# Two more tiles turned on VectorE in the first half of layer 0

## The chip, the cores and the metric

The kernel runs on one core of one Trainium2 chip. The metric is the device time of one execution in microseconds (us); lower is better. Times of the kernel before are the median of three runs.

## What is computed

Two layers, each a linear-attention block and an MLP with residuals, on 2048 tokens of width 448 in float32 (16 heads of 28, hidden width 1792):

```python
x = x + A(layernorm(x), wqkv, wo)      # A: phi(t) = where(t > 0, t + 1, exp(t)) + 1e-6
x = x + B(layernorm(x), w1, b1, w2, b2)  #   kv = phi(k)^T v, z = sum phi(k)
x = x + A(layernorm(x), wqkv, wo)      #   o = (phi(q) kv) / (phi(q) z + 1e-6), then @ wo
x = x + B(layernorm(x), w1, b1, w2, b2)  # B: gelu(x @ w1 + b1) @ w2 + b2
```

## The kernel before

The 2048 tokens are 16 tiles of 128. Products keep float32's accuracy by splitting each operand into a high and a low part ("hi" and "lo", XH and XL for the normalised input) and adding three products. A layer has a first half (a pass over the 16 tiles that makes the keys, the queries and the sum G), a transition, and a second half (queries and MLP in blocks of four tiles). The change touches the first half of layer 0 only.

Instructions are issued in an order written out by hand: for each tile t, `STEPS` gives a string of tokens, or else `STEP`, and `phase1` issues what each token names, on whichever engines it needs. Every engine works off its own queue in that order. The tokens:

- `qp`: phi of the queries made a step earlier (ScalarE relu and exp into eq, VectorE adds, L372; then a store to memory by SP). `K`, `Q`: the products for keys and queries of tile t, 11 matmuls each on TensorE (L353). `Q` is issued in the first half for tiles up to 8.
- `a`, `n`: layer norm of a later tile: statistics (VectorE L209, L221, L214, then GpSimd's power brs, L215) and normalisation (VectorE L442).
- `T`: where a tile's transposition is on TensorE, the four transposes of tile t+1 into PSUM (L264). For these tiles `stage_n` also copies the tail of the row (ScalarE, L446).
- `v` with a number, or `tu`: where it is on VectorE, `turn` transposes the tile in 32x32 squares (L303, L304) into a buffer that holds two tiles. After the odd one, SP stores the pair to memory (`store_sq`, L310). `sp`: SP spreads each stored pair back into SBUF by four DMAs (L318), so that the squares come to lie where a full transpose would have put them.
- `X`: split of tile t+1 into XH (ScalarE) and XL (VectorE): from PSUM `split_x` (L276, L277), from the spread squares `split_t` (L335, L336).
- `s`: split of the normalised tile itself, the stationary side of G (ScalarE xnh L477, GpSimd xnl L478 and a short L479).
- `kp`, `kh`, `kl`: phi of the keys (ScalarE ek L369, L370, VectorE L372), its high part (ScalarE L517), its low part and the running sum za (VectorE L526, L533).
- `G`: the 11 matmuls of tile t-1 into G (L622). `bg`: casts of MLP weights that were loaded a step earlier (ScalarE w1h, w1x; GpSimd w1l), then loads of the next pieces by SP. `ld`: the load of a later x tile by SP.

`TURNED[l]` is the first tile of layer l that VectorE turns; tiles below it use TensorE's transposes. It is 8 in layer 0 and 0 in layer 1. `k_at`, `q_at` and `g_at` say at which of the 11 places the matmuls with the low part stand, so that they come when that part is there; `merge` puts the list together. The psk and tp/psq banks come in pairs ("m" and "h", two buffers each), used in turn; the buffers for stored and spread squares and some weight pieces are five of one kind ("S").

Of the kernel before, what the change touches and what calls it, by code (L numbers as in the profile page):

```python
# [22 lines left out]
def linear_attn_mlp_kernel(  # L23
# [12 lines left out]
    pe, act, dve, pool, sp = nc.tensor, nc.scalar, nc.vector, nc.gpsimd, nc.sync  # L36
# [8 lines left out]
    G = 112  # L45
# [37 lines left out]
    def load_x(l, t):  # L83
        xt[l, t] = t448("H", 8, f"x{l}_{t}")
        sp.dma_start(xt[l, t], x_d[l][t * 128:(t + 1) * 128, :])
# [166 lines left out]
    def block(key):  # L252
        if key not in blocks:
            blocks[key] = Block(APART if key[0] == "a" else 0)
        return blocks[key]
# [3 lines left out]
    def transpose_x(xn, tail, key, j, tag="m"):  # L259

        block(key)
        tp = tps[key, j] = bank(tag, 4 if tag == "acc" else 2, "tp")
        for c in range(4):
            pe.transpose(tp[:, c * 128:(c + 1) * 128], xn[:, c * 128:(c + 1) * 128] if c < 3 else tail, ident)  # L264
# [8 lines left out]
    def split_x(key, j):  # L273
        tp = tps.pop((key, j))
        hi, lo = blocks[key].pieces(j)
        act.copy(hi, tp)  # L276
        dve.tensor_sub(lo, tp, f(hi))  # L277
# [20 lines left out]
    def turn(x, key, t):  # L298
        x = x[:, :D]
        if (key, t // 2) not in squares:  # L300
            squares[key, t // 2] = half("sq")
        sq = squares[key, t // 2].rearrange("p (m c u n) -> p c m u n", m=4, c=4, n=32)[:, :, :, t % 2]
        dve.transpose(sq[:, :3], x[:, :TL].rearrange("p (c m n) -> p c m n", c=3, n=32))  # L303
        dve.transpose(sq[:, 3].rearrange("p (u m) n -> p u m n", u=2),  # L304
                      x[:, TL:].rearrange("p (m n) -> p m n", n=32)[:, None].to_broadcast([128, 2, 2, 32]))
# [70 lines left out]
    def bg_pieces():  # L376
        n = 0
        both = []

        def stage():  # L380
            nonlocal n
            n += 1
            if n <= LATE:
                k = (n - 1) // 2
                if k % 2 == 0 or k > 5:
                    return t512("xn", 2, "stg")[:, :D]

                if n % 2:
                    both.append(half("stg"))
                return both[-1][:, n % 2 * 512:][:, :D]  # L390
            return t448(f"W{5 + n % 2}", 1, "stg")

        for fc in range(4):
            sl = slice(fc * D, (fc + 1) * D)
            for c in range(4):
                s = stage_piece(w1[:, sl], c, sp, stage())

                def go(c=c, s=s, sl=sl):
                    if c < 3:
                        act.copy(w1h[:, c, sl], s)  # L400
                        pool.tensor_tensor(w1l[:, c, sl], s, f(w1h[:, c, sl]), op=OP.subtract)
                    else:
                        act.copy(w1x[:, sl], s)
                        pool.tensor_tensor(w1x[64:128, sl], s[64:128], f(w1x[64:128, sl]), op=OP.subtract)
                yield go
        for i in range(NF):
            s = stage()
            sp.dma_start(s, w2[i * 128:(i + 1) * 128, :])

            def go(i=i, s=s):  # L410
                act.copy(w2h[:, i], s)
                pool.tensor_tensor(w2l[:, i], s, f(w2h[:, i]), op=OP.subtract)
            yield go

    bg = bg_pieces()
# [14 lines left out]
    sts = {}  # L430


    TURNED = (8, 0)
    tails = {}

    def stage_a(l, t):
# [2 lines left out]
    def stage_n(l, t):  # L439
# [3 lines left out]
        xns[l, t] = xs  # L443
        if t < TURNED[l]:
            d = tails[l, t] = b2b[:, t % 2 * 128:][:, :128]
            act.copy(d.rearrange("p (u n) -> p u n", u=2), xs[:, None, TL:].to_broadcast([128, 2, 64]))  # L446

    def stage_t(l, t):
        if t >= TURNED[l]:
            turn(xns[l, t], ("a", l, t // 4), t % 4)  # L450
            if t % 2:
                store_sq(("a", l, t // 4), t % 4 // 2)

    def stage_sp(l, t):
        if t >= TURNED[l]:
            block(("a", l, t // 4))
            spread(("a", l, t // 4), t % 4 // 2)

    def stage_b(l, t, tag="h"):
        if t < TURNED[l]:  # L460
            transpose_x(xns[l, t], tails.pop((l, t)), ("a", l, t // 4), t % 4, tag)
# [4 lines left out]
    def stage_x(l, t):  # L466
        key = ("a", l, t // 4)
        if t < TURNED[l]:
            split_x(key, t % 4)
# [13 lines left out]

    def k_at(l, t):
        if t < 9:
            return (3, 6, 9, 11) if t == 0 or l == 0 and 2 < t < 8 else (2, 5, 8, 11)
        return (2, 5, 8, 11) if t == 9 else (1, 4, 7, 10)

    def q_at(l, t):
        if t < 9:  # L490
            return (2, 5, 8, 11) if l == 0 and t < 7 else (2, 4, 7, 10) if t == 0 else (1, 4, 7, 10)
        return {11: (4, 7, 10, 11), 12: (5, 7, 9, 11),
                13: (5, 8, 10, 11), 15: (1, 5, 8, 11)}.get(t, (1, 4, 7, 10))

    def g_at(l, t):
        if t < 9:
            return (4, 7, 10) if l == 0 and 0 < t < 6 else (3, 6, 9)
        return (2, 5, 8) if t < NT - 1 else (2, 6, 9)

    def stage_k(l, t, cs=range(4)):  # L500
        ko[l, t] = proj("k", ("a", l, t // 4), t % 4, ko.get((l, t)), cs, k_at(l, t))
# [47 lines left out]
    def stage_q(l, t, cs=range(4), tag=None):  # L549
        if tag:  # L550
            qs_[l, t] = bank(tag, 4, "psq")[:, :D]
        qs_[l, t] = proj("q", ("a", l, t // 4), t % 4, qs_.get((l, t)), cs, q_at(l, t))
        if 3 in cs:
            qo.append((l, t, qs_.pop((l, t))))
# [33 lines left out]
    def stage_qphi(n=9):  # L588
        for _ in qo[:n]:
            l, t, o = qo.pop(0)  # L590
            if (l, t) == (0, 0):
                by_rs(o)

            e = phi(o, "eq", tag="e" if t < NT - 2 else "E")
            sp.dma_start(pq_d[l][t * 128:(t + 1) * 128, :], e)

    def fill_qphi():

        l, t, o = qo.pop(0)
        e = t512("e", 3, "eq")[:, :D]  # L600
        p = t512("E", 2, "ep")[:, :D]
        act.activation(e, o, AF.Relu, scale=-1.0)
        act.activation(p, o, AF.Relu)
        act.activation(e, e, AF.Exp, scale=-1.0)
        pool.tensor_tensor(e, p, e, op=OP.add)
        sp.dma_start(pq_d[l][t * 128:(t + 1) * 128, :], e)

    def stage_g(l, t, acc, mid=lambda: None):
        h, lo = split.pop((l, t))
        kh, kl = ks.pop((l, t))  # L610
        first, last = t == 0, t == NT - 1
        x = [h[:, c * 128:(c + 1) * 128] for c in range(3)] + [h[:, TL:]]
        his = [(c, x[c], k) for c in range(4) for k in (kh, kl)]
        if t == NT - 3:
            his = his[::2] + his[1::2]
        los = [(c, lo[:, c * 128:(c + 1) * 128], kh) for c in range(3)]
        made = merge(his, los, g_at(l, t))
        for i, (c, w, k) in enumerate(made):
            if i == 3:
                mid()  # L620
            others = [m[0] for m in made[:i]], [m[0] for m in made[i + 1:]]
            pe.matmul(acc[c], w, k, start=first and c not in others[0], stop=last and c not in others[1])  # L622
# [17 lines left out]
    STEPS = {  # L640
# [9 lines left out]
    }  # L650
    NORM = (
# [122 lines left out]
    def trans_gt(tr, acc):  # L774
        tr.gt = []
        for c in range(4):
            s = t512("A" if c < 2 else "B", 2, "gt")[:, :D]
            act.copy(s, acc[c])
            tr.gt.append(s)
# [52 lines left out]
    def load_pq(l, b, j):  # L832
        t = b * 4 + j
        pqt[l, t] = t448(f"W{j}", 1, f"pq{l}_{t}")
        sp.dma_start(pqt[l, t], pq_d[l][t * 128:(t + 1) * 128, :])
# [280 lines left out]
    for l in range(LAYERS):  # L1116
# [11 lines left out]
        def pre(j):  # L1128
# [6 lines left out]
            Q=lambda j: stage_q(l, fill.pop(0)), Qp=lambda j: fill_qphi(), Qv=lambda j: stage_qphi(j or 9),  # L1135
# [3 lines left out]
            ld=lambda j: (load_pq(l, 0, j), load_x(l, j)), gt=lambda j: trans_gt(tr, acc),  # L1139
# [14 lines left out]
        for b in range(NB):  # L1154
# [6 lines left out]
            for i in range(NF):  # L1161
# [12 lines left out]
                elif l + 1 < LAYERS:  # L1174
# [4 lines left out]
                    if i in (3, 4, 6, 7, 8):  # L1179
                        t = (3, 4, 6, 7, 8).index(i)  # L1180
# [36 lines left out]
```

## Time and profile before

| | us |
|---|---|
| median of 3 runs (866.61 to 866.7) | 866.67 |
| the profiled execution | 866.77 |
| span of its trace | 865.0 |
| TensorE busy | 859.5 (99%) |
| VectorE busy | 489.9 (57%) |
| ScalarE busy | 354.0 (41%) |
| GpSimd busy | 209.1 (24%) |

The page names TensorE PE (its weight loads PEld), VectorE DVE, ScalarE ACT, GpSimd POOL and the DMA queue of SyncE SPq. Times in a timeline are from the start of the span. The granted TensorE clock was at full speed in all slices. The first half of layer 0 lies at about 7 to 105 us.

### The profile page before, as it was taken

Reading aid. Unit: us, or ns where it says so; the run is one execution under the profiler, and the core shown is the slowest. Engines: PE = TensorE matmul, PEld = TensorE weight load, DVE = VectorE, ACT = ScalarE, POOL = GpSimd, SP = SyncE. Lnnn points to the kernel's source line nnn. Section 1 sums busy time; section 2 is a strip of 40 time slices with the busy share of each in tenths; the row PEclk is TensorE's granted clock in tenths of the full one; section 3 lists DMA queues with packets and bytes.
Section 4 is the critical chain, followed back from the end, with each engine's and each line's share of the span. In section 5 each row is a group of like instructions: output and inputs, shape, how many; then the busy total and the mean of one; then the engine's idle time right before and its main releaser. Section 6 shows DMA issues by size and latency. Waiting matters only on the chain.

```text
span 865.0 us, 11671 instructions
## 1 busy us (share of the span) xinstructions
PE 859.5 (99%) x4173; PEld 769.9 (89%) x4173; DVE 489.9 (57%) x956; ACT 354.0 (41%) x634; POOL 209.1 (24%) x242
## 2 busy tenths in 40 slices
PE   9999999999999999999999999999999999999998
PEld 8999988888888888888899998988888888888887
DVE  7888676559455443236477877664674383533112
ACT  6776656333323322333356565632232233223231
POOL 3565612235013012012222343120220140140000
PEclk9999999999999999999999999999999999999999
DMA  5475546633313502051145543362332423111001
GB/s 168 131 241 178 187 112 206 194 112 109 135 60 114 150 0 98 1 182 49 49 149 187 164 129 97 108 217 81 116 107 91 135 74 114 50 49 42 1 1 43
DMA packets 65082, 95.81 MB, mean 111 GB/s; under 512 B 9088, under 2 KB 59904, under 8 KB 65024
## 3 DMA queue, kind: packets, MB, share of 16 engines
q1 hardware_dynamic: 63696, 94.13, 33.8%
q10 hardware_dynamic: 1328, 0.93, 0.4%
q8 instruction: 33, 0.54, 0.3%
q14 instruction: 25, 0.20, 0.1%
HBM read 56.70 MB, written 35.13 MB: 106 GB/s over the span
## 4 chain that ended last, share of the span: by engine, by line
PE 95%; ACT 2%; DMA 1%; DVE 1%; issue 0%; POOL 0%; ACTq 0%; SPq 0%; DVEq 0%
PE hp L972 31%; PE y L1002 10%; PE y L1001 10%; PE y L1003 10%; PE G L622 8%; PE psk L353 8%; PE psq L353 5%; PE op L891 2%; PE op L890 2%; PE op L892 2%; DMA sp<-sq_m 1%; PE op L880 1%; PE op L879 1%; PE op L881 1%; PE kvp L786 1%; PE mp L796 1%
## 5 line engine op out<-in xcount | busy, mean ns | idle before, releaser
L978 DVE TENSOR_TENSOR gl<-g,gh 128x512 fp32r<-128x512 f32 x112 | 83.2, 743 | 293.2 <-ACT gh L977 293.2
L974 ACT ACTIVATE g<-hp,b1s 128x512 f32<-128x512 f32 x112 | 77.1, 688 | 400.1 <-PE hp L972 400.1
L1002 PE MATMUL y<-w2l,gh 128*128 128x448 f32 x447 | 163.6, 366 | 0.0
L1001 PE MATMUL y<-w2h,gh 128*128 128x448 f32 x447 | 162.2, 363 | 0.0
L1003 PE MATMUL y<-w2h,gl 128*128 128x448 f32 x447 | 160.3, 359 | 0.1
L972 PE MATMUL hp<-XH,w1h 128*128 128x512 f32 x336 | 130.7, 389 | 0.0
L972 PE MATMUL hp<-XH,w1l 128*128 128x512 f32 x336 | 130.7, 389 | 0.0
L972 PE MATMUL hp<-XL,w1h 128*128 128x512 f32 x336 | 130.1, 389 | 0.0
L215 POOL TENSOR_TENSOR brs<-bve,mhalf 128x1 f32<-128x1 f32 x55 | 34.8, 632 | 258.4 <-DVE bve L214 257.9
L1001 PEld LDWEIGHTS y<-w2h,gh 128*128 128x128 f32 x447 | 83.7, 187 | 9.8 <-ACT gh L977 0.5
L1002 PEld LDWEIGHTS y<-w2l,gh 128*128 128x128 f32 x447 | 83.9, 188 | 6.9
L1003 PEld LDWEIGHTS y<-w2h,gl 128*128 128x128 f32 x447 | 84.0, 188 | 5.8 <-DVE gl L978 0.9
L972 PEld LDWEIGHTS hp<-XL,w1h 128*128 128x128 f32 x336 | 63.1, 188 | 13.1
L972 PEld LDWEIGHTS hp<-XH,w1h 128*128 128x128 f32 x336 | 63.0, 187 | 10.7
L972 PEld LDWEIGHTS hp<-XH,w1l 128*128 128x128 f32 x336 | 63.1, 188 | 9.9
L977 ACT CAST gh<-g 128x512 fp32r<-128x512 f32 x112 | 69.6, 622 | 3.6
L840 POOL TENSOR_TENSOR pz<-pq,zb 128x448 f32<-128x448 f32 x32 | 37.0, 1162 | 103.3 <-DVE dn L846 67.1
L353 PE MATMUL psk<-wk,XH 128*128 128x448 f32 x210 | 61.8, 364 | 0.0
L353 PE MATMUL psq<-wq,XH 128*128 128x448 f32 x196 | 57.5, 366 | 0.0
L478 POOL TENSOR_TENSOR xnl<-x,xnh 128x384 fp32r<-128x384 f32 x32 | 35.0, 1092 | 69.3 <-ACT xnh L477 56.0
L622 PE MATMUL G<-kh,xnh 128*128 128x448 f32 x128 | 46.8, 368 | 0.0
L336 DVE TENSOR_TENSOR XL<-sp,XH 128x512 fp32r<-128x512 f32 x54 | 45.3, 851 | 2.1 <-ACT XH L335 2.1
(185 smaller groups left out, 1491.1 us busy)
## 6 DMA issues: line engine op xcount, KB each, us to landing
x<-in_A_x_dram SPq DMA_DIRECT2D x32, 224.0 KB, 3.7
pq_d<-eq SPq DMA_DIRECT2D x32, 224.0 KB, 2.7
pq<-pq_d SPq DMA_DIRECT2D x32, 224.0 KB, 3.1
sq_m<-sq SPq DMA_DIRECT2D x14, 512.0 KB, 2.6
x<-x_d SPq DMA_DIRECT2D x32, 224.0 KB, 3.7
sp<-sq_m SPq DMA_DIRECT2D x52, 128.0 KB, 2.8
sq_a<-sq SPq DMA_DIRECT2D x12, 512.0 KB, 2.9
sp<-sq_a SPq DMA_DIRECT2D x48, 128.0 KB, 2.7
```

Of the source, the lines that this page charges most:

```text
L336: eng.tensor_tensor(lo.rearrange("p (c i n) -> p c i n", c=4, n=32), x, f(h), op=OP.subtract)
L353: pe.matmul(o, x, p, start=(i == 0), stop=(i == 10))
L478: pool.tensor_tensor(lo[:, :TL], xn[:, :TL], f(h[:, :TL]), op=OP.subtract)
L622: pe.matmul(acc[c], w, k, start=first and c not in others[0], stop=last and c not in others[1])
L840: pool.tensor_tensor(pz, pqt[l, b * 4 + j], tr.zb, op=OP.mult)
L972: pe.matmul(o, w, r, start=(k == 0), stop=(k == len(made) - 1))
L974: act.activation(g, hp, AF.Gelu_apprx_tanh, bias=b1s[:, i:i + 1])
L977: act.copy(gh, g)
L978: dve.tensor_sub(gl, g, f(gh))
L1001: pe.matmul(acc[j], gh[:, s], w2h[:, i], start=first, stop=False)
L1002: pe.matmul(acc[j], gh[:, s], w2l[:, i], start=False, stop=False)
L1003: pe.matmul(acc[j], gl[:, s], w2h[:, i], start=False, stop=stop)
```

## The change

`TURNED` of layer 0 goes from 8 to 6, so tiles 6 and 7 are turned by VectorE, stored and spread, and TensorE's four transposes for each of them and the two tail copies go. The bounds in `k_at`, `q_at` and `g_at` move with it: tiles 6 and 7 in K, 5 and 6 in Q, and 4 and 5 in G take the positions that the later tiles have. The steps of tiles 3 to 11 are written anew. Normalisation of tiles 6 and 7 and statistics of tile 8 change places within steps 3 and 4, so that 6 and 7 can be turned at the end of step 3. The turns of tiles 9 to 15 each come a step later, and the spreads move with the stores. In steps 5 to 8 `X`, the split of the next tile, stands behind `s`, and in all of steps 5 to 11 ahead of `kp`. In steps 6, 9, 10 and 11 a turn stands directly ahead of `kp`, in steps 7 and 8 directly behind it.

```diff
-    TURNED = (8, 0)
+    TURNED = (6, 0)
...
     def k_at(l, t):
         if t < 9:
-            return (3, 6, 9, 11) if t == 0 or l == 0 and 2 < t < 8 else (2, 5, 8, 11)
+            return (3, 6, 9, 11) if t == 0 or l == 0 and 2 < t < 6 else (2, 5, 8, 11)
...
     def q_at(l, t):
         if t < 9:
-            return (2, 5, 8, 11) if l == 0 and t < 7 else (2, 4, 7, 10) if t == 0 else (1, 4, 7, 10)
+            return (2, 5, 8, 11) if l == 0 and t < 5 else (2, 4, 7, 10) if t == 0 else (1, 4, 7, 10)
...
     def g_at(l, t):
         if t < 9:
-            return (4, 7, 10) if l == 0 and 0 < t < 6 else (3, 6, 9)
+            return (4, 7, 10) if l == 0 and 0 < t < 4 else (3, 6, 9)
...
     STEP = "qp K T X s a kp n kh kl tu G bg Q ld sp"
     STEPS = {
         (0, 1): "T X a3 q1 s kh n3 kl q1 G bg ld",
         (0, 2): "K T X s a4 kp n4 a5 kh kl n5 a6 G bg Q ld",
-        (0, 3): "qp K T X s a7 kp kh n6 kl a8 G bg Q ld",
-        (0, 4): "qp K T X s a9 kp kh n7 n8 kl n9 v8 v9 G bg Q ld sp",
-        (0, 8): "qp K T X s a kp n kh kl tu a14 G bg Q ld sp",
-        (0, 9): "qp K T X s kp n14 kh kl v14 G bg",
-        (0, 10): "K T X s a15 kp n15 kh kl v15 G bg sp",
-        (0, 11): "K T X kp s kh kl G bg",
+        (0, 3): "qp K T X n6 s a7 kp kh n7 kl v6 v7 G bg Q ld sp",
+        (0, 4): "qp K T X s a8 kp kh n8 a9 kl v8 n9 G bg Q ld",
+        (0, 5): "qp K s X kp kh v9 a10 kl n10 G bg Q ld sp",
+        (0, 6): "qp K s X v10 kp kh a11 kl n11 G bg Q ld",
+        (0, 7): "qp K s X kp v11 kh a12 kl n12 G bg Q ld sp",
+        (0, 8): "qp K s X kp v12 kh a13 kl n13 a14 G bg Q ld",
+        (0, 9): "qp K X s v13 kp n14 kh kl G sp bg",
+        (0, 10): "K X s v14 kp a15 kh kl n15 G bg",
+        (0, 11): "K X v15 kp s kh kl G sp bg",
         (1, 0): "K T X s kp kh kl a n tu Q ld sp",
     }
```

## The prediction

> **What bounds the kernel now.** I read the page first, then TensorE's waits over the whole run, then the chain that ended last through layer 0's first half, then the timelines of the engines and queues around tiles 3 to 14.
>
> ```profile
> PE 859.5 (99%) x4173; PEld 769.9 (89%) x4173; DVE 489.9 (57%) x956; ACT 354.0 (41%) x634; POOL 209.1 (24%) x242
> PE warm L170 <- DVE one L164: 1.1, 1, 1.1
> PE psk L567 <- ACT wk L137: 0.8, 1, 0.8
> ```
>
> The first line is the page's busy time; the other two are all of TensorE's waits. TensorE bounds the kernel. Its only waits, 1.1 and 0.8 us, lie in the launch, ahead of everything that the diff touches. So there is no idle time for the change to remove: it can only take TensorE work away, or bring a wait in.
>
> ```profile
> 42.98 0.44 PE tp L264 x4
> 43.41 2.21 PE G L622 x11
> 45.62 2.20 PE psq L353 x11
> 50.03 0.44 PE tp L264 x4
> 50.47 2.21 PE G L622 x11
> ```
>
> These are pieces of the chain (start, us, what). Between K, G and Q pieces of 2.2 us stand the four transposes of tile 6 (42.98, in step 5) and of tile 7 (50.03, in step 6), 0.44 us each, with nothing idle around them.
>
> **What is removed.** Both pieces go: 2 x 0.44 = 0.88 us of TensorE, all on the path. That is the whole possible gain, and 0.10% of the run. Differences within 0.2% (1.7 us) count as no change here, about what a measurement of this kernel can tell. The matmuls' changed order inside K, Q and G keeps their number and shapes, so it costs nothing by itself. ScalarE also loses the two copies of the tails (about 0.2 us of queue each).
>
> **What is added.** Each tile is now turned in squares on VectorE, stored, spread back by four DMAs, and split from SBUF instead of PSUM.
>
> ```profile
> 42.48 0.57 DVE L303 STREAM_TRANSPOSE sq<-x 128x384 f32<-128x384 f32 x1
> 43.82 0.58 DVE L372 SCALAR_TENSOR_TENSOR eq<-psq,eq 128x448 f32<-128x448 f32 x1
> L336 DVE TENSOR_TENSOR XL<-sp,XH 128x512 fp32r<-128x512 f32 x8 | 8.2, 1027 | 0.8 <-ACT XH L335 0.8
> L277 DVE TENSOR_TENSOR XL<-tp,XH 128x512 fp32r<-128x512 f32 x5 | 3.4, 683 | 0.8 <-ACT XH L276 0.8
> 74.47 1.02 POOL L478 TENSOR_TENSOR xnl<-x,xnh 128x384 fp32r<-128x384 f32 x1
> 74.60 1.43 DVE L336 TENSOR_TENSOR XL<-sp,XH 128x512 fp32r<-128x512 f32 x1
> ```
>
> Two tiles were turned from 42.48 to 43.82, 0.67 us each, so VectorE gains 1.34 us. The groups between 20 and 105 us show an XL from SBUF at 1027 ns on average against 683 from PSUM. The last two lines say why: XL of tile 11 began just after GpSimd's xnl and ended 0.54 us after it (76.03 against 75.49). I take "held until GpSimd is done" as a hazard of up to 1.43 - 0.65 = 0.8 us for each such operation. In steps 5 to 8 xnh now stands ahead of the next tile's XH, so xnl starts some 0.6 us before XL, and a hold becomes the rule.
>
> The TensorE work is gone for certain; the cost is whether operands still arrive in time. I follow the new queue order through three places.
>
> **Place 1: step 3, the bank for Q of tile 4.**
>
> ```profile
> 31.10 0.68 DVE L277 TENSOR_TENSOR XL<-tp,XH 128x512 fp32r<-128x512 f32 x1
> 31.54 1.02 POOL L478 TENSOR_TENSOR xnl<-x,xnh 128x384 fp32r<-128x384 f32 x1
> 31.70 0.62 DVE L209 BATCH_NORM_STATS2 bst<-x 128x6 f32<-128x448 f32 x1
> 32.64 0.62 DVE L372 SCALAR_TENSOR_TENSOR psk<-psk,ek 128x448 f32<-128x448 f32 x1
> 33.17 0.50 DVE L442 TENSOR_SCALAR x<-x,bmv,brs 128x448 f32<-128x448 f32 x1
> 33.29 0.64 ACT L517 ACTIVATE kh<-psk,tiny 128x448 fp32r<-128x448 f32 x1 [0.77 <-DVE psk L372]
> 33.96 0.62 DVE L526 SCALAR_TENSOR_TENSOR kl<-psk,kh 128x448 fp32r<-128x448 f32 x1 [0.29 <-ACT kh L517]
> 35.03 0.62 DVE L209 BATCH_NORM_STATS2 bst<-x 128x6 f32<-128x448 f32 x1
> 35.53 0.58 ACT L370 ACTIVATE eq<-eq 128x448 f32<-128x448 f32 x1
> 36.14 0.62 DVE L372 SCALAR_TENSOR_TENSOR eq<-psq,eq 128x448 f32<-128x448 f32 x1
> 38.40 0.37 PE L353 MATMUL psq<-wq,XH 128*128 128x448 f32 x1
> ```
>
> The order was XL4, statistics of 7, phi of 3, n6, kl3, za, statistics of 8, eq; it becomes XL4, n6, statistics of 7, phi of 3, n7, kl3, za, turns of 6 and 7, eq. n6 would start at 31.70, where xnl runs until 32.56; held, it ends at about 33.0. The statistics take 32.64 - 31.70 = 0.94, so phi starts at 33.94, 1.3 us late (0.45 if n6 isn't held). kh and all of ScalarE behind it shift by that, less the tail copy: the exp that ended at 36.11 ends at about 37.2. n7 fits into the wait for kh. kl starts at 35.27, kl and za take 35.03 - 33.96 = 1.07, two turns 1.34: eq starts at 37.68 and ends at 38.30, where it ended at 36.76. Q of tile 4 reuses, by the two-bank rotation, the bank that this eq reads, and starts at 38.40. So 1.64 us of cover become 0.1: cost 0, up to 0.3 if something slips. Statistics of 8 move from step 3's end into step 4 and change VectorE's total by nothing.
>
> **Place 2: tile 6 by way of memory, and G of tile 5.**
>
> ```profile
> 79.78 0.27 DVE L304 STREAM_TRANSPOSE sq<-x 128x128 f32<-128x128 f32 x1
> 80.08 0.32 SPq L310 DMA_DIRECT2D sq_a<-sq  x1
> 83.03 1.76 SPq L318 DMA_DIRECT2D sp<-sq_a  x4
> 87.37 0.62 ACT L335 CAST XH<-sp 128x512 fp32r<-128x512 f32 x1 [0.88 <-DMA sp<-sq_a]
> 88.02 0.69 DVE L336 TENSOR_TENSOR XL<-sp,XH 128x512 fp32r<-128x512 f32 x1 [0.79 <-ACT XH L335]
> 47.66 0.56 PE L353 MATMUL psk<-wk,XH 128*128 128x448 f32 x2
> 50.51 0.36 PE L622 MATMUL G<-kl,xnh 128*128 128x448 f32 x1
> DMA to landing us min/median/max: 2.5/2.9/3.8
> 31.58 0.47 SPq L103 DMA_DIRECT2D stg<-in_B_w_dram  x1
> 40.46 0.56 ACT L403 CAST w1x<-stg 128x448 fp32r<-128x448 f32 x1
> 44.34 1.15 SPq L101 DMA_DIRECT2D stg<-in_B_w_dram  x2
> 47.54 0.57 ACT L400 CAST w1h<-stg 128x448 fp32r<-128x448 f32 x1 [0.39 <-DMA stg<-in_B_w_dram]
> ```
>
> Tiles 14 and 15 price the detour: store issued at 80.08, four spreads at 83.03, XH of tile 14 released at 87.37: 7.29 us. The new store goes out at 37.7, so XH of tile 6 can start at 45.0 and XL ends at 46.3, or 47.1 if held. K of tile 6 moves from 47.66 to 47.22 and fits. Behind that XH stands ek of tile 5 (0.5 for XH, 1.15 for relu and exp): phi of 5 at 46.65, then on VectorE phi 0.53, turn of 9 0.67, statistics of 10 0.94, kl 0.62: ends at 49.4. G of tile 5 wants kl at 50.51 - 0.88 = 49.63. Cost 0 to 0.25 (with XL held).
>
> On SP the store stands ahead of the loads that went out from 31.58, so these now leave after 38.0; such a load took 47.54 - 44.34 = 3.2 us, and ScalarE's w1x cast slides from 40.46 to about 41.9, the w1h cast behind it to 42.6, and eq of tile 4 behind both is ready at 44.2 (0.47 for the cast, 1.15 for relu and exp). VectorE comes to that eq at 44.0: 37.68, then eq 0.6, XL 0.65, statistics of 8 0.94, phi 0.53, n8 0.45, statistics of 9 0.94, kl and za 1.07, turn 8 0.67, n9 0.45. So it costs 0.2 of VectorE's time and nothing on TensorE; were VectorE on time as before, it would be more. By the same sum kl of 4 ends at 42.4, ahead of its G, which moves from 43.41 to 42.97. The x loads behind are used a step or more later.
>
> **Place 3: steps 9 to 13, XL of tile 14.**
>
> ```profile
> 76.73:81.15 4.42, 4.42 (x24) 4.13 (x23) 4.20 (x10) 3.17 (x6) 2.03 (x3) 1.00 0.07 27
> 89.97 0.37 PE L353 MATMUL psk<-wk,XL 128*128 128x448 f32 x1
> ```
>
> Without Q a step is 4.42 us, and VectorE (third busy time of the windows' line) fills 4.20 of it. Here turns 13, 14 and 15 come a step later, and turn 15 now stands behind XL of tile 12 instead of ahead of it. Turn 15 ended at 80.05; XL of 14 ended at 88.71, 8.66 later, and K of 14, which starts with XL, came at 89.97: cover 1.26. Now TensorE comes at 89.09. Following the order with 0.65 for an XL, 0.67 a turn, 0.94 statistics and the ScalarE waits as before, turn 15 ends at 80.1; with one hold of 0.8, at 81.0. XL of 14 then ends at 88.75 to 89.65: TensorE waits 0 to 0.55.
>
> **The sum.** Waits do not add: one at an early place moves the later needs back. So -0.88 and 0 to 0.55; I take 0.1, near the lower end, because the larger one needs a hold just there. The profiled execution took 866.77 (span 865.0 and 1.77 around it), 0.10 above the median 866.67. 866.77 - 0.88 + 0.1 = 866.0 there, 865.9 as median.
>
> **Rivals.** (A) The detour is slower than tiles 14 and 15 show. Landings went from 2.5 to 3.8 around a median of 2.9, so store and spread could come up to 1.8 later together; with 1.5, phi of 5 starts at 48.15, kl ends at 50.9, and G of 5 waits 1.27: 866.67 - 0.88 + 1.27 = 867.1. For it: ScalarE's queue holds ek of 5 behind XH of 6. Against: no transposed tile's data was late but the last pair's, by 0.88 of ScalarE's time.
>
> (B) VectorE becomes the bound in steps 9 to 11, and the run is slower. Place: XL of 10, 11, 12 and n14, n15, held by GpSimd, 0.8 each: 4.0 us, turn 15 at 84.1. K of 14 then waits 84.1 + 8.66 - 89.09 = 3.67: 869.5. It starts to cost when turn 15 ends after 80.43, and makes the run slower by over 0.2% when it ends after 83.04. For it: 4.20 of 4.42 us busy, and 1.34 us more work upstream with 0.88 us less time. Against: the 4.20 hold such delays already (XL of 11 alone 0.8), and before step 9 VectorE still has gaps. The Trainium skill speaks for (B)'s side: VectorE: DVE Perf Modes, sections "The three transpose paths" and "Rules for kernel authors", has VectorE turn only 32x32 blocks and sends a full 128x128 transpose to TensorE. By that rule 0.44 us of TensorE are the cheaper way and the result is a loss such as (B)'s, not a gain of 0.88; the rows agree about the detour's 7.29 us, not yet that it ends up on the path.
>
> (C) Faster by over 0.2%: needs 0.85 us beyond the removed pieces, and no wait of TensorE is there to remove.
>
> That the change does not remove the transposes is excluded: in the built kernel's order tiles 6 and 7 have none.
>
> **Chances and range.** Forecast 0.56 (865.8 to 866.4), (A) 0.18, (B) 0.24, (C) 0.02. The forecast and (A) lie within 0.2%: 0.74; slower 0.24; faster 0.02. (B) is given more than the replay alone bears, since the cover is at 0.1 to 0.5 us in four places and I follow queues by hand. The range goes from 865.6 (all 0.88, and the 0.1 by which runs differ on both sides) into (B), to 868.6.
>
> **What would show it.** Right: the chain has no tp pieces at 43 and 50, K of tile 12 starts 0.6 to 0.9 earlier, TensorE's list has at most 0.6 us of new waits, on XL of 14, on kl of 5 or on eq ahead of Q of 4. Store of 6 and 7 near 37.7, XH of 6 near 45.0, turn 15 ending by 81. Wrong: a wait of over 1 us on XL or kl between 38 and 95, turn 15 after 83, or a wait at a place not named.

## The result and the profile after

| | before | after |
|---|---|---|
| median of nine runs (us) | 866.70 (866.44 to 867.34) | 869.41 (867.09 to 870.59) |
| the profiled execution (us) | 866.77 | 870.35 |
| its span (us) | 865.0 | 868.5 |

The ratio after to before is 1.0025, 95% interval 1.0013 to 1.0036: slower, by 2.7 us in the medians. A later set of eleven runs (a2, below) gave 867.94 against 867.03, ratio 1.0013 [1.0004, 1.0023]. The runs of the changed kernel spread over more than 3 us, those of the kernel before over 0.9 us.

The page's busy times of after, and then all of TensorE's waits (what waited, for what; us in total, times, longest):

```profile
PE 860.4 (99%) x4165; PEld 769.2 (89%) x4165; DVE 492.4 (57%) x960; ACT 353.0 (41%) x632; POOL 210.4 (24%) x242
```

```profile
PE psk L353 <- DVE XL L336: 2.0, 2, 1.6
PE warm L170 <- DVE one L164: 1.1, 1, 1.1
PE psk L567 <- ACT wk L137: 0.7, 1, 0.7
PE G L622 <- DVE kl L526: 0.5, 1, 0.5
```

The eight transposes are gone (4165 matmuls for 4173). In their place stand three waits that before did not have: on the keys' low part of tile 5 and twice on XL, 2.5 us together. The timeline of after shows these places and what stands behind them on ScalarE and VectorE (start, us, engine, line; in brackets the idle time before it and who ended it; the first three lines are TensorE's):

```profile
50.83 0.47 PE L622 MATMUL G<-kl,xnh 128*128 128x448 f32 x1 [0.45 <-DVE kl L526]
73.31 0.47 PE L353 MATMUL psk<-wk,XL 128*128 128x448 f32 x1 [0.40 <-DVE XL L336]
93.10 0.47 PE L353 MATMUL psk<-wk,XL 128*128 128x448 f32 x1 [1.63 <-DVE XL L336]
46.30 0.62 ACT L335 CAST XH<-sp 128x512 fp32r<-128x512 f32 x1 [1.13 <-DMA sp<-sq_a]
71.80 0.62 ACT L335 CAST XH<-sp 128x512 fp32r<-128x512 f32 x1 [2.11 <-DMA sp<-sq_a]
80.94 0.62 ACT L335 CAST XH<-sp 128x512 fp32r<-128x512 f32 x1 [1.09 <-DMA sp<-sq_a]
91.70 0.62 ACT L335 CAST XH<-sp 128x512 fp32r<-128x512 f32 x1 [3.26 <-DMA sp<-sq_a]
92.35 0.69 DVE L336 TENSOR_TENSOR XL<-sp,XH 128x512 fp32r<-128x512 f32 x1 [3.17 <-ACT XH L335]
```

ScalarE stands before XH four times because the spread squares have not landed (1.13 + 2.11 + 1.09 + 3.26 = 7.6 us; before it did so once, for 0.88), and VectorE stands idle behind it. The landing time (from a transfer's issue to its arrival) of all stores and spreads of layer 0's first half, from the view of the buffer in memory between 30 and 100 us:

```profile
DMA to landing us min/median/max: 2.5/3.9/5.3
```

Before had 2.5/2.9/3.8.

The chain that ended last shows how one pair hangs on another (start, us, what):

```profile
38.04 2.90 DMA sq_a<-sq
42.33 3.87 DMA sp<-sq_a
46.30 0.62 ACT XH L335
46.92 0.45 ACT ek L369
48.00 0.63 DVE psk L372
49.33 2.91 DMA sq_a<-sq
53.58 4.52 DMA sp<-sq_a
59.10 1.47 DVE XL L336
61.82 3.17 DMA sq_a<-sq
66.37 5.33 DMA sp<-sq_a
71.80 0.63 ACT XH L335
73.96 2.58 DMA sq_a<-sq
77.87 3.04 DMA sp<-sq_a
82.99 2.87 DMA sq_a<-sq
87.20 4.48 DMA sp<-sq_a
91.70 0.63 ACT XH L335
92.35 0.70 DVE XL L336
93.10 2.49 PE psk L353 x11
```

Where before the chain was TensorE's own from 30 to 105 us, it now goes through all five pairs: store, spread, XH, then XL or the phi behind it, the next pair's turn, its store (behind the fourth pair it passes through the normalisation n15 on VectorE, which ended at nearly the same time as that pair's XH). From the store's issue to XH's start the first pair took 46.30 - 38.04 = 8.26 us and the fifth 91.70 - 82.99 = 8.71 (before: 7.29); the three between took 8.77, 9.88 and 6.95 to the landing of their last spread (53.58 + 4.52 - 49.33 for the second).

This execution also began K of tile 4 0.56 us later than that of before (34.11 against 33.55). Of that, 0.51 us stand already at K of tile 3 (26.92 against 26.41), with which the first rewritten step begins, so nearly all of it comes from the launch; the times below are read with it. So the spans' 3.5 us come about: 0.56 from there, -0.88 from the transposes, 0.6 + 0.6 + 1.8 in the three gaps (each is 0.15 to 0.2 longer than the wait listed, from one matmul's start plus 0.2 to the next one's), 0.35 in small gaps around tiles 11 to 13, 0.24 behind the stage; 0.2 are spread over the rest.

### The profile page after: what moved, and what is told of

It reads as the page before. It is cut to its first block, busy times and chain, and to the rows that moved or that the text cites. A ratio compares the mean times of both kernels' runs of the same rounds, so it can differ in the third digit from the quotient of the medians.

```text
span 868.5 us, 11673 instructions
## 1 busy us (share of the span) xinstructions
PE 860.4 (99%) x4165; PEld 769.2 (89%) x4165; DVE 492.4 (57%) x960; ACT 353.0 (41%) x632; POOL 210.4 (24%) x242
## 4 chain that ended last, share of the span: by engine, by line
PE 88%; DMA 5%; DVE 3%; ACT 2%; issue 1%; SPq 1%; POOL 1%; ACTq 0%; DVEq 0%; POOLq 0%
PE hp L975 32%; PE y L1005 10%; PE y L1004 10%; PE y L1006 10%; PE G L622 5%; PE psk L353 5%; PE psq L353 4%; DMA sp<-sq_a 2%; PE op L894 2%; DMA sq_a<-sq 2%; PE op L893 2%; PE op L895 2%; PE op L883 1%; PE op L882 1%; PE op L884 1%
## 5 line engine op out<-in xcount | busy, mean ns | idle before, releaser
L336 DVE TENSOR_TENSOR XL<-sp,XH 128x512 fp32r<-128x512 f32 x56 | 47.1, 852 | 7.7 <-ACT XH L335 7.7
L622 PE MATMUL G<-kl,xnh 128*128 128x448 f32 x128 | 46.2, 366 | 0.5 <-DVE kl L526 0.5
```

Source lines behind the costliest of these rows:

```text
L336: eng.tensor_tensor(lo.rearrange("p (c i n) -> p c i n", c=4, n=32), x, f(h), op=OP.subtract)
```

## Experiments

Before was run beside all of them: median 866.87 for e1 to e4, 866.86 for f1 to f4, 867.03 for a2, g1, g2 and h1, 866.75 for h2, h3, g3 and i1. Ratios are to it. Unless said otherwise, edits are to the changed kernel.

### Does the way through memory cost the time, or VectorE?

Two theories: (D) the data come back from memory too late; (V) VectorE itself falls behind, held by GpSimd.

**e1**: the split of all pairs reads the turned squares directly; stores and spreads run as before, but nobody waits for them.

```diff
         sq = squares.pop((key, h))
+        if key[:2] == ("a", 0):
+            kept[key, h] = sq
...
-        x = spreads[key, t // 2]
+        x = kept.get((key, t // 2), spreads[key, t // 2])
```

> In the changed kernel every pair of tiles that VectorE turns in the first half of layer 0 is still stored and spread, but the spread lands in a place that nobody reads, and the split takes the squares themselves (so the keys and queries of tiles 6 to 15 are computed from wrongly placed squares). Theory D (the way through memory lands too late): all of TensorE's new waits go, and the time is 866.7 - 0.9 = 865.8, with runs within 0.5 us of each other. Theory V (VectorE, held by GpSimd, is late by itself): the same instructions stand in the same order on VectorE and GpSimd, so the time stays near 869.4.

Measured: 866.22 (865.67 to 866.86), ratio 0.9989 [0.9981, 0.9998]. TensorE has no wait behind the launch, while stores and spreads landed in 2.5/3.1/4.3. So (D) holds and (V) is refuted: the same work on VectorE, in the same order, with the wait for memory gone, is 0.65 us faster than before, near the 0.88 of the removed transposes. The runs lie within 1.2 us of each other, not 0.5. Two other ways in which the edit could have helped are not seen in its profile: XL from the squares took 1023 ns in the mean (998 from the spreads in after), and ScalarE's waits for weight pieces were 0.6 and 0.5 us (0.6 and 0.6 in after).

**e2**: the same for the last pair (14 and 15) alone.

> The same for the last pair alone (tiles 14 and 15 are split from the squares themselves, so their keys and queries are not the reference's). In the profile of the changed kernel K of tile 14 came 1.8 us late, the largest of its waits. Theory D: that wait goes, the others (0.7 us on kl of tile 5, 0.6 on XL of tile 10) stay: 869.4 - 1.8 = 867.6, and still runs that differ by 1 us or more. Theory V: 869.4.

Measured: 867.43, ratio 1.0002 [0.9993, 1.0011]. The last pair's wait is gone and that on kl of tile 5 stays (0.6 us), as (D) said; the one on XL of tile 10, which was to stay too, is not in this profile.

**e3**: the new order without the new detour: `TURNED = (8, 0)`, and `T` stands in steps 5 and 6 again.

> The new order of the steps with tiles 6 and 7 left on TensorE (TURNED is 8 again; T comes back in steps 5 and 6). It costs the 0.9 us of transposes again and has no detour for tiles 6 and 7; tiles 8 to 15 are turned as late as in the changed kernel. Theory D with the lateness handed down from pair to pair, beginning with tile 6: the chain starts on time, 866.7 to 867.5. Theory D with each pair late for itself, because it is turned a step later: 868 to 869.5, the waits on XL of 10 and 14 as before. Theory V: about 869.

Measured: 867.16, ratio 1.0004 [0.9995, 1.0012]; no new wait of TensorE in layer 0's first half. The order alone costs nothing that can be told from zero; it harms together with the pair 6/7.

### Which place, and is the lateness handed on?

Theory (L): the lateness starts at the first pair and passes from pair to pair; (S): each detour is slow by itself.

**f4**: e1's edit for the pair 6/7 only.

> The changed kernel with tiles 6 and 7 alone split from their squares themselves (store and spread still run, unread; their keys and queries are not the reference's). Theory L: the lateness that the first pair hands down is gone, so that kl of 5 is on time and the later pairs leave up to 2 us earlier: 866.0 to 867. Theory S: only the wait on kl of 5 goes, 868.7.

Measured: 866.53 (865.56 to 868.38), ratio 0.9998 [0.9989, 1.0006]; in the range of (L). But its profile, of an execution of 867.80, still has 0.8 us of waits on XL in layer 0's first half, and ScalarE waits 5.1 us for the spreads: the later pairs can be late without the first one.

**f2**: in step 5 the keys' phi stands ahead of the split, as before the change.

```diff
-        (0, 5): "qp K s X kp kh v9 a10 kl n10 G bg Q ld sp",
+        (0, 5): "qp K s kp X kh v9 a10 kl n10 G bg Q ld sp",
```

> In step 5 of the changed kernel alone, the split of tile 6 stands behind the phi of tile 5's keys (kp X kh v9 instead of X kp kh v9). Both theories: the wait of about 0.7 us on kl of tile 5 goes, since ek of tile 5 no longer queues behind XH of tile 6 on ScalarE. Theory L: the loop stays, and v9 still comes behind XL of 6, so the waits on XL of 10 and 14 stay or grow by what the earlier wait gave them: 868.7 to 869.4. If the first wait were the whole cause, it would be 866.

Measured: 866.79 (865.72 to 868.51), ratio 1.0003 [0.9994, 1.0012]; well under the 868.7 to 869.4 of (L), and nearer to the 866 that was given for the first wait as the whole cause.

**f1**: turns 9, 11, 13 and 15 each ahead of the next tile's split, so that a late pair does not hold back the next pair's store.

```diff
-        (0, 5): "qp K s X kp kh v9 a10 ...
+        (0, 5): "qp K s v9 X kp kh a10 ...
# the same in steps 7, 9 and 11
```

> In steps 5, 7, 9 and 11 of the changed kernel the turn that completes a pair (tiles 9, 11, 13, 15) stands ahead of the split X of the next tile instead of behind it. Theory L (a loop: XL of the pair before must be done before VectorE turns the next pair's second tile, its store and spread follow, and so lateness passes from pair to pair every two steps): the squares of 8 to 15 leave 2 to 4 us earlier, the waits on XL of 10 and 14 go, the wait on kl of tile 5 stays: 866.7, at most 867. Theory S (each detour is slow for itself): the chain is as long as before and TensorE waits as in the changed kernel, 869.

Measured: 868.14 (866.78 to 869.23), ratio 1.0015 [1.0006, 1.0024]. A miss for (L) as I had put it.

```profile
37.66 0.33 SPq L310 DMA_DIRECT2D sq_a<-sq  x1
46.23 0.38 SPq L310 DMA_DIRECT2D sq_a<-sq  x1
48.74 0.53 SPq L101 DMA_DIRECT2D stg<-in_B_w_dram  x1
51.19 1.75 SPq L318 DMA_DIRECT2D sp<-sq_a  x4
```

These lines of SP's timeline in f1 say why (`stg` is a weight piece): the second store left at 46.23, 3.1 us sooner than in the changed kernel, but its spreads only at 51.19, because the store itself took 4.9 us to land (2.9 in the changed kernel); the loads between them had all left by 49.75. And the first pair was later than in the changed kernel: its spreads landed in 4.0 to 5.6 us (3.5 to 4.1 there), and TensorE waited 0.7 us for XH of tile 6.

**f3**: f1 and f2 together (in step 5 `v9 kp X`).

> Both edits together: the turns ahead of the splits in steps 5, 7, 9 and 11, and phi of tile 5 ahead of the split of tile 6. Theory L: no wait of TensorE is left but those of the launch, 866.7 - 0.9 = 865.8 to 866.2, faster than both kernels. Theory S: 868.5.

Measured: 867.39 (865.67 to 869.64), ratio 1.0007 [0.9998, 1.0016]; not faster than both kernels, as (L) had it. In its profile (an execution of 866.68, span 864.9) TensorE waits nowhere in layer 0's first half; what its executions of up to 869.64 wait for is not recorded.

What follows: two edits at the first place alone, one of the data (f4) and one of an order (f2), each take back most of the loss, though TensorE's direct wait there was 0.45 us. So the first place starts much of it, at ScalarE: XH of tile 6 waits there for memory, and ek of tile 5 stands behind it. How the lateness passes on from there (phi of 5, turn 9, a weight cast) is not shown. f1 was to break the path between pairs without touching the first place and took back nothing, but since its first pair landed later too, it does not tell (L) from (S).

### Can SP's order put it right?

**e4**: in steps 3, 5 and 7 the spreads go out ahead of the weight loads (`G sp bg Q ld`).

> In steps 3, 5 and 7 of the changed kernel the four spreads stand on SP ahead of the weight loads and the x load instead of behind them; nothing else moves. If the spreads land late because those loads are queued ahead of them and share the DMA engines, their landing falls from a median of 3.9 us towards 2.9 and the time to 867 to 868; the weight casts come later and may cost ScalarE up to 1 us. If the landing is late for another reason, the time stays at 869.4.

Measured: 875.83, ratio 1.0107 [1.0091, 1.0122], much worse. Landings fell to 2.5/2.8/4.0 as forecast (the spreads of pair 6/7, now ahead of the loads, to 2.7 to 3.4 us from 3.5 to 4.1), but now the weights are late, and their casts hold ScalarE. ScalarE's and TensorE's timeline:

```profile
47.03 0.57 ACT L403 CAST w1x<-stg 128x448 fp32r<-128x448 f32 x1 [6.31 <-DMA stg<-in_B_w_dram]
50.14 0.64 PE L353 MATMUL psk<-wk,XH 128*128 128x448 f32 x1 [2.76 <-ACT XH L335]
```

And e4's windows (stretch, its length, busy time of PE, PEld, DVE, ACT and POOL, then TensorE's granted clock, DMA share, GB/s):

```profile
47.00:50.00 3.00, 0.37 (x2) 0.01 (x1) 0.62 (x1) 2.94 (x7) 2.20 (x2) 1.00 0.76 262
52.00:55.00 3.00, 3.00 (x9) 2.65 (x9) 2.93 (x9) 2.81 (x6) 1.22 (x2) 0.50 0.43 178
57.00:60.00 3.00, 3.00 (x16) 2.78 (x15) 2.93 (x9) 0.64 (x1) 1.95 (x3) 0.98 0.82 231
```

ScalarE's wait for one weight piece made K of tile 6 wait 2.76 us, and that gap brought a second loss: the clock was granted at 0.50 until about 57 us.

**g2**: f3, and in steps 5 and 7 the spreads ahead of only the second of the two weight loads (the one that waits for GpSimd).

```diff
-  ... G bg Q ld sp"
+  ... G b1 sp b2 Q ld"
```

> The turns of tiles 9, 11, 13 and 15 stand ahead of the next tile's split, and in steps 5 and 7 the spreads stand ahead of that weight load which waits for GpSimd. Under the theory that the lateness is handed from pair to pair and that SP's order adds to it: 865.9 to 866.6, near the run in which nothing waits for memory (866.22). If the spreads ahead of a load cost as much as in the run that put them ahead of both loads: over 868.

Measured: 867.97 (866.61 to 870.54), ratio 1.0012 [1.0003, 1.0022]; a miss. Now an x load, behind the spreads, is what comes late (VectorE's and TensorE's timelines):

```profile
70.12 0.63 DVE L209 BATCH_NORM_STATS2 bst<-x 128x6 f32<-128x448 f32 x1 [0.91 <-DMA x<-in_A_x_dram]
73.58 0.47 PE L353 MATMUL psk<-wk,XL 128*128 128x448 f32 x1 [2.25 <-DVE XL L336]
```

Neither reordering of SP's queue removes the lateness; each hands it to another load.

### Does the landing time hang on the traffic?

**a2**: the changed kernel once more.

> The changed kernel itself once more, beside the three below on one chip. Theory: the way through memory is late by a few tenths to three microseconds at the steps of tiles 5, 9 and 13, by how long the stores and spreads take to land in that execution. Expected 869.4 us, single runs between 867 and 871, with the waits of TensorE again on the keys' XL of tile 5, the split of tile 10 and the split of tile 14, in other proportions than before.

Measured: 867.94 (866.75 to 869.88), ratio 1.0013 [1.0004, 1.0023]. Its profiled execution took 867.21, with landings of 2.4/3.3/4.3 and a single wait of TensorE behind the launch, on kl of tile 5:

```profile
PE G L622 <- DVE kl L526: 0.6, 1, 0.6
```

Of the three waits forecast, only the first appeared. The spreads of pair 6/7 landed in 3.3 to 4.1 us, much as in the first profile of this kernel (3.5 to 4.1); some later ones came sooner (those of pair 8/9 in 3.4 to 4.0 us against 4.7 to 4.8).

**h1**: ten stores of 229 KB that nobody reads, one behind each of ten weight loads.

```diff
                 s = stage_piece(w1[:, sl], c, sp, stage())
+                if 4 <= n <= 13:
+                    sp.dma_start(dram([128, D], F32, f"more_{n}"), f(wkq["k", 0][0]))
```

> The changed kernel with one more store of 229 KB, which nobody reads, behind each of ten weight loads (the fifth to the fourteenth), so that the 16 DMA engines carry more between about 30 and 100 us. If the landing time of the stores and spreads hangs on the traffic beside them, their median rises from 3.9 us to 4.5 or more and the time by 1 to 4 us over the changed kernel's (870.5 to 873.5). If it does not, the median stays within 0.5 us and the time within 0.5 us.

**h2**: the same edit to the kernel before.

> The kernel before with the same ten unread stores as h1. If the 4.6 us of h1 came through the way through memory, which here only tiles 14 and 15 go, with 0.9 us of waiting in the kernel before: 867 to 868.5. If the stores cost time by themselves (they hold back the weight loads or SP's queue): 870 or more.

**h3**: the same edit to e1.

> e1 (no pair waits for memory, 866.22) with the same ten unread stores as h1. If the harm comes through the wait for the pairs: 866 to 867, though the landing median rises over e1's 3.1 us. If the stores cost by themselves: 869 or more.

| pairs that the splits wait for | without the stores | with them | difference | landing without / with |
|---|---|---|---|---|
| five (a2, h1) | 867.94 | 872.56, 1.0065 [1.0052, 1.0078] | 4.6 | 2.4/3.3/4.3, 2.5/3.9/6.4 |
| four (before, h2) | 866.75 | 868.91, 1.0027 [1.0016, 1.0038] | 2.2 | 2.5/2.9/3.8, 2.5/3.1/5.8 |
| none (e1, h3) | 866.22 | 867.29, 1.0006 [0.9997, 1.0015] | 1.1 | 2.5/3.1/4.3, 2.5/4.3/5.6 |

From h1's profile, TensorE's waits in layer 0's first half:

```profile
PE psk L353 <- DVE XL L336: 3.6, 3, 2.1
PE psk L353 <- ACT XH L335: 1.9, 1, 1.9
PE G L624 <- DVE kl L528: 0.7, 1, 0.7
```

These are the changed kernel's places again, and ScalarE's wait for the spreads is 12.3 us there (4.9 in a2). h1's time came as expected; the landing median did not reach 4.5, and it is no higher than in after's first profile. h2 and h3 were above what I expected, by 0.4 and 0.3 us. My expectation of h2 also had the kernel wrong: before sends four pairs through memory (tiles 8 to 15), and only the last was awaited in its profile.

The medians mix pairs that travel beside the extra stores with pairs behind them, so I read the spreads pair by pair (landing in us, shortest to longest of the four):

| pair | a2 | h1 | before | h2 | e1 | h3 |
|---|---|---|---|---|---|---|
| 6/7 | 3.3 to 4.1 | 4.6 to 6.4 | | | 3.6 to 3.9 | 4.6 to 5.0 |
| 8/9 | 3.4 to 4.0 | 4.7 to 4.9 | 2.8 to 3.8 | 4.7 to 4.9 | 2.9 to 3.5 | 4.9 |
| 10/11 | 4.2 to 4.3 | 4.7 to 6.0 | 3.0 to 3.6 | 5.6 to 5.8 | 3.8 to 3.9 | 5.4 to 5.6 |
| 12/13 | 2.5 to 3.0 | 2.5 to 3.2 | 2.5 to 2.9 | 2.7 to 3.1 | 2.5 to 3.0 | 2.5 to 3.1 |

The last of the extra stores leaves at 64 to 68 us, well ahead of the spreads of pair 12/13 (at 74 to 81 us). The pairs whose spreads travel beside the extra stores land later with them than without; pair 12/13 comes at most 0.2 us later. These are single profiles, and after's first one had 4.7 to 4.8 us for pair 8/9 with no extra store; but for pair 6/7 only one of twelve profiles without them (f1) reaches the times with them. So more traffic makes the way through memory longer. What the wait for the pairs adds is h1 against h3, where only that wait differs: 4.6 us against 1.1 (4.5 against 1.5 by the ratios). h2 does not belong on that line. The one wait of TensorE in layer 0's first half in its profile (1.7 us on XL of tile 10) goes back to an x load that left at 67.25, behind the extra stores, and landed 4.7 us later, not to a split that waited for its pair.

The Trainium skill (DMA: Bandwidth & Descriptors, section "Latency and other measured facts") has HBM's access at 0.2 us on average and 2 us at high load, which goes the same way: the largest landing of h2 is 2.0 us above before's. Why the later pairs of the changed kernel land differently in two executions is open.

### A version that beats both?

**g1** has the phi ahead of the split in steps 5 to 8; **g3** is the same again; **i1** is g1 with turn 15 ahead of the split in step 11.

```diff
-        (0, 6): "qp K s X v10 kp kh a11 ...
+        (0, 6): "qp K s kp X v10 kh a11 ...
# i1 too:
-        (0, 11): "K X v15 kp s kh kl G sp bg",
+        (0, 11): "K v15 X kp s kh kl G sp bg",
```

g1:

> The steps of tiles 5 to 8 have the keys' phi ahead of the next tile's split again, as the kernel before has it; steps 9 to 11 stay as changed. In step 5 alone this gave 866.79. If ScalarE's order at step 5 was the only harm of that order, the other three steps change nothing: 866.6 to 867.0. If the split standing ahead harms in steps 6 to 8 too (phi waits there behind a split that waits for memory), 866.0 to 866.4. If the split ahead helps there, as the change would have it, over 867.3.

g3:

> g1 once more (the phi ahead of the split in steps 5 to 8). 866.41 was 0.6 under the kernel before in the median, with three of eleven runs over 867.3. If that is real: 866.2 to 866.6 and most runs under the kernel before's median; if it was the draw of landing times: 866.7 to 867.3.

i1:

> g1 with the turn of tile 15 ahead of the split of tile 12 in step 11, so that the last pair's store leaves about 1.2 us sooner. The one wait that g1's profile shows is 0.21 us on the split of tile 14. Expected 866.0 to 866.5 with fewer runs over 868; if the split of tile 12 gets late by it, 867 or more.

Measured: g1 866.41 (865.70 to 868.64), 0.9997 [0.9988, 1.0006]; g3 866.80 (865.63 to 868.22), 1.0003 [0.9994, 1.0012]; i1 866.66 (866.28 to 866.91), 0.9998 [0.9989, 1.0007]. g3 says that g1's low median was the draw; i1 came 0.2 us above what I expected. i1's eleven runs lie within 0.63 us where g1's and g3's spread over 2.9 and 2.6, which would fit a last pair that no longer comes late in some executions; its profile still has 0.5 us of waits on XL. All three are level with before. Over all, the five kernels with the phi first in step 5 and SP's order kept (f2, f3, g1, g3, i1) have ratios of 0.9997 to 1.0007, those with the split first there (after, a2, f1) 1.0013 to 1.0025; the intervals of single ones overlap. Nothing that really waits for the pairs beat the kernel before.

## Why the prediction was wrong

Forecast 865.9, range 865.6 to 868.6; measured 869.41. That is outside the range, on its slow side, and where a small gain was forecast there was a loss; the second set's 867.94 lies inside the range, but it too is slower than before.

**The removal was right.** No tp pieces in the chain at 43 and 50, and e1 shows the gain: 0.65 us in the medians, where 0.88 was counted.

**Place 1 was right.** VectorE's and TensorE's timelines of after:

```profile
37.94 0.58 DVE L372 SCALAR_TENSOR_TENSOR eq<-psq,eq 128x448 f32<-128x448 f32 x1
39.00 0.37 PE L353 MATMUL psq<-wq,XH 128*128 128x448 f32 x1
```

eq ended at 38.52 and Q of tile 4 started at 39.00 without a wait: cover 0.48, not 0.1, since with the late launch taken off, eq started 0.3 us sooner than forecast.

**Place 2 is the step that failed: the price of the detour.** I took 7.29 us from one pair, 14 and 15, which in that profile ran at the end of the stage, and let it stand for a pair sent out at 38 us. Pair 6/7 took 38.04 to 46.30, 8.26 us, 0.97 more. The profile of before had four pairs to take the price from: from the store's issue to the landing of the last spread they took 8.1, 7.8, 7.1 and 7.2 us, and I used the last. With about 0.1 us from landing to XH, the first one's price gives kl of 5 at 50.3 by the same working, and a wait of 0.7 us, where 0.45 (after) and 0.6 (a2) were measured.

What made the spreads of pair 6/7 slow is what stands ahead of them on SP. The prediction saw that the store holds back three weight loads and an x load, so that they leave after 38.0, but charged them only to ScalarE's casts. They left at 38.42 to 40.34, just ahead of the spreads at 41.00, whose last took 3.87 us to land; e4, with the spreads ahead of the loads, had 2.7 to 3.4. The windows' DMA share of 42 to 48 us (the number before the last) shows how full this time became, 0.54 before and 0.94 after:

```profile
42.00:48.00 6.00, 6.00 (x33) 5.60 (x32) 5.74 (x14) 3.71 (x7) 3.33 (x5) 1.00 0.54 183
42.00:48.00 6.00, 6.00 (x31) 5.62 (x30) 3.70 (x9) 4.13 (x8) 4.16 (x5) 1.00 0.94 299
```

What followed at that place is the mechanism of rival (A): XH of 6 late, ek of 5 behind it, phi of 5 at 48.00 (forecast 46.65; 47.44 with the late launch taken off), kl of 5 late for its G. (A) said 867.1 for that, and a2's profiled execution, where this is the only new wait, took 867.21; that the numbers agree is in part luck, since (A) had a wait of 1.27 us and a2's was 0.6. Its share of the chances, 0.18, was too small: the longer way was in the rows of before, and the cover was 0.2 us.

**Place 3 failed with it, and by the same term.** I let only GpSimd's holds push turn 15, took "the ScalarE waits as before", and kept 8.66 us from the turn's end to XL of 14; the pairs 8/9, 10/11 and 12/13 I did not follow through memory at all. In after, turn 15's store left at 82.99 (forecast for the turn's end 80.1 to 81.0) and XL of 14 ended at 92.35 + 0.70 = 93.05, 10.1 us later, because the detour took 8.71. Turn 15 was late mainly because XH of 10 had waited 2.11 us for its pair: XL of 10 started only at 72.45, and from there to turn 15 VectorE was busy nearly all the time and could not catch up. The wait of 1.09 ahead of XH of 12 did not add to it, for VectorE was at n15 until 81.66, when that XH had ended at 81.56. Holds by GpSimd did occur. XL took up to 1.47 (at 59.10), but in the mean no more than before, where the group's mean was 1027 ns; normalisations took 771 ns in the mean for 642, but 810 in e1, where TensorE waited for nothing:

```profile
L336 DVE TENSOR_TENSOR XL<-sp,XH 128x512 fp32r<-128x512 f32 x10 | 10.0, 998 | 6.3 <-ACT XH L335 6.3
```

So rival (B), the one nearest in time (869.5), had the place, XL of 14, but not the mechanism: VectorE was idle for 3.17 us ahead of that XL, and 6.3 us in all ahead of XLs, for XHs that waited for memory. That its number is so near is luck: it had one wait of 3.67 us there, and after had 1.63 there and two more elsewhere.

**The sum was wrong in form.** I wrote that waits do not add. In after they did: 0.45 + 0.40 + 1.63 at kl of 5, XL of 10 and XL of 14, against 0.88 removed. An early wait of TensorE moves its later needs back, but the late data moved the later pairs' stores back as well, so the later waits did not become free. f4 shows how much hangs on the first pair: relative to before, the kernel goes from 1.0025 (1.0013 in the second set) to 0.9998.

**The rule that was cited.** The prediction set the Trainium skill (VectorE: DVE Perf Modes, sections "The three transpose paths" and "Rules for kernel authors") against the change: a full transpose belongs on TensorE. For tiles 6 and 7 the result sides with the rule, by another reason than a slow VectorE: e1 shows the squares as such to be the cheaper way, and the way that puts them in place costs more than the 0.88 us saved.

## What to carry to other kernels

A round trip through memory is priced at the place and beside the traffic where it will run: of several in the profile take the one nearest in place, and look at which other transfers the change moves next to it. If the cover is smaller than the spread of the landings, count the wait as likely. Then look at what stands behind the waiting instruction in its engine's own queue: here a split that waited for memory held back a phi of another tile, and putting the phi first took back most of the loss. Where one late transfer holds back the next one's start, the waits along that chain can add up; do not take the largest alone.

## What was not expected of the hardware

How long a transfer took depended on its place in the kernel. The spreads of 128 KB of pair 12/13 landed in 2.5 to 3.2 us in all eighteen profiles; those of pair 6/7 took 3.1 to 5.6 in the twelve that have them behind the loads and without extra stores, 4.6 to 6.4 with extra stores, and 2.7 to 3.4 in e4. Stores of 512 KB mostly landed in 2.6 to 3.3 us, but pair 8/9's took 6.0 in g2, where it left at 44.96, and 4.9 in f1 (46.23); in after and a2, where it left at 48.8 to 49.3, it took 2.9. After a TensorE gap of 2.76 us in e4 its clock was granted at 0.50 for some 7 us, and matmuls followed each other every 0.37 us instead of 0.20; gaps of 1.6 us in after and 2.25 us in g2 left it at 1.00. The Trainium skill (TensorE: Matmul & The Clock Gate, section "Part 1: The HAM clock gate") puts the fall to half the clock behind an idle window of about 3.4 us; the run agrees on the half, but e4's gap was shorter than that.
